# Seven block products for the up projection of two chunks, from the third token tile on

## The chip, the cores and the metric

One core of a Trainium2 chip runs the whole kernel. Its engines have instruction streams of their own and wait for one another by semaphores: TensorE (PE) multiplies and writes PSUM, with weight loads (PEld) beside the matmuls; VectorE (DVE), ScalarE (ACT) and GpSimd (POOL) do elementwise work, of which DVE and ACT read PSUM here; SyncE (SP) issues the DMAs. The metric is device microseconds of one execution, lower is better.

## The reference

Two softmax attentions (32 packed queries gather keys and values, then 576 queries read the packed result), the real part of a two-dimensional FFT, a layer norm, and a two-layer network with a ReLU:

```
p_packed = sm_attn(p, k, v)                    # 8 batches, 8 heads, 576 tokens, 64 per head
x = sm_attn(q, p_packed, p_packed)             # then (8, 576, 512)
mixed = np.real(np.fft.fft(np.fft.fft(x, axis=1), axis=2))
u = x + mixed
un = (u - mean(u)) / np.sqrt(var(u) + 1e-06)
out = u + np.maximum(un @ w_ch1, 0.0) @ w_ch2  # 512 -> 2048 -> 512
```

The change is in `un @ w_ch1` and in what surrounds it.

## The kernel before

The 4608 tokens are 36 blocks of 128, taken as nine tiles (t = 0 to 8) of 512. `front(b)` makes `u` of one batch: attention, FFT as matrix products, layer norm statistics. `ffn` runs the two-layer network of one tile. The 2048 hidden features are 16 chunks j of 128.

For each chunk `up` (L638) runs 12 matmuls of 128x512 into the PSUM bank `ph`, four blocks of 128 input features times three terms: each fp32 operand is a high and a low part (`uh`, `ul` for tokens, `wr_h`, `wr_l` for weights), and high·high, low·high and high·low are added. ACT makes `hh` = ReLU of `ph` (L644), DVE the low part `hl` (L645). `down` of the chunk before (L655) runs 12 matmuls into the four banks `acc0` to `acc3`. `wsplits` gives a weight chunk its high part on ACT (L101) and low part on POOL (L102), for w1 and w2, in every tile anew.

`step(i)` stands at two places in every chunk and runs the next piece of the front of batch t+1, in the order of the letters in `ORDER`, so that front and network of the tile before share the engines: `pz`, `py`, `px` are the front's FFT products (L228 to L230, L526), `pg`, `po`, `s`, `s2T`, `e1tp` its other PSUM results. Its PSUM tiles come from `bank`: three buffers of pool `ps`. From tile 1 on the order of PE, DVE, ACT and POOL is as the code is written (`manual_schedule`); in tile 0 a scheduler orders it. The front of batch 7 is issued in tile 6, its last pieces in tile 7, and tile 8 has none.

At the end of a tile the tokens of the next are centred (`less`, L592), transposed (L599, 16 matmuls into `untp`) and split into `uh` and `ul` by `parts`; `acc` times 1/σ plus `u` (L691) is the result, and SP stores it (L692). The PSUM has eight banks of 512 fp32: three of `ps`, `ph`, four `acc`.

Of the kernel before, what the change touches and what calls it, by code (L numbers as in the profile page):

```python
# [17 lines left out]
P = 128  # L18
S = 576
HS = S // 2  # L20
D = 64
# [21 lines left out]
         "y f1 r1 h1",  # L43
         "S y X y p0 p1 y d0 d1 y g0 y U y g1 y e0 y e1 y y m0 y a0 y m1 y a1 y f0 y r0 y h0 y f1 y r1 y "
         "h1 y y")

# [3 lines left out]
LEAD = 2  # L50
NJ = 16
MANUAL = {getattr(mybir.EngineType, n) for n in ("PE", "DVE", "Activation", "Pool")}
NE = 289
# [26 lines left out]
def tile_kernel(ctx, tc, kpT, qT, v, w1, w2, tabs, tabR, tabB, tabT, sel, ident_d, out):  # L80
# [6 lines left out]
    small = ctx.enter_context(tc.tile_pool(name="small", bufs=2))  # L87
    ps = ctx.enter_context(tc.tile_pool(name="ps", bufs=3, space=bass.MemoryType.PSUM))
    psf = ctx.enter_context(tc.tile_pool(name="psf", bufs=1, space=bass.MemoryType.PSUM))

    spare = ["acc0", "acc1", "acc2", "acc3"]
# [18 lines left out]
    for h in range(4):  # L110
        nc.gpsimd.memset(bmask[h * NPK:(h + 1) * NPK, h:h + 1], 0.5)
    w1f = cpool.tile([P, NJ, DM], F32, name="w1f")
    w2f = cpool.tile([P, NJ, DM], F32, name="w2f")

    nc.scalar.activation(small.tile([P, 1], F32, tag="ri", name="warm"), mhalf, AF.Exp)
    ubuf = cpool.tile([P, NU, DM], F32, name="ubuf")
    stages = (STG0 + STG1 * 40)[:2 * NJ]

# [24 lines left out]
    def spot(n, part, shape):  # L143

        t = (w1f, w2f)[n].rearrange("p j n -> p (j n)")[:, (part % NJ) * DM:]
        size = shape[1] * shape[2]
        return t[:, 0:size].rearrange("p (a n) -> p a n", a=shape[1])
# [12 lines left out]
    def load_weights(j):  # L160

        for n, dst in enumerate((w1f, w2f)):
# [5 lines left out]
            c = dst[:, j, :].bitcast(I32)  # L168
# [63 lines left out]
    def front(b):  # L232
# [56 lines left out]
        def turned_scores(*gs):  # L289
# [12 lines left out]
            for g in gs:  # L302
# [3 lines left out]
                rinv[g] = ri  # L306

        def packed(g):

# [42 lines left out]
        def queries(*gs):  # L352

            for g in gs:
                if g not in qts:
                    load_queries(g)

            tails = [bank("s2Tt")] + ([psf.tile([P, 512], F32, tag="ph", name="s2Tt")] if len(gs) == 2 else [])
            s2T = narrow(gs, lambda g, h: ppT[g][side(g, h):side(g, h) + D, h * NPK:(h + 1) * NPK],
                         lambda g, h, w: qts[g][side(g, h):side(g, h) + D, h // 2, w], "s2T", dict(zip(gs, tails)))  # L360
            for g in gs:
                s2s[g] = work.tile([P, 18, 32], F32, tag="att", name="s2", bufs=ATT)
            for c, w in ((1, slice(16, 18)), (0, slice(0, 16))):
                for g in reversed(gs):
                    nc.vector.transpose(s2s[g][:, w, :].rearrange("p a k -> p (a k)"), s2T[g][c])

        def less_one(g):
# [97 lines left out]
        def folded_parts(g):  # L465
# [12 lines left out]
        parts = {"S": lambda _: scores(0, 1), "U": lambda _: queries(0, 1), "X": lambda _: turned_scores(0, 1),  # L478
                 "s": scores, "t": turned_scores, "p": packed, "d": packed_parts, "q": queries, "e": less_one, "m": less_mean, "g": values_spectrum, "a": weights, "f": folded, "r": folded_rest,
                 "h": folded_parts,  # L480
# [10 lines left out]
        yh, yl, yr = [], [], []  # L491
        for t, base in enumerate((0, FO)):
            nr = NRC[t]
            hi = work.tile([P, 2, N2], F32R, tag="att", name="yh", bufs=ATT)
            lo = work.tile([P, 2, N2], F32R, tag="att", name="yl", bufs=ATT)
            for c in range(2):
                py = bank("py")
                for g in range(2):
                    w = slice(base + c * P, base + (c + 1) * P)
                    three(py[:, :N2], fh[g][:, w], fl[g][:, w], gh[g][:, t, :], gl[g][:, t, :], g == 0, g == 1)  # L500
                split(hi[:, c, :], lo[:, c, :], py[:, :N2])
            py = bank("pyr")
            for g in range(2):
                w = slice(base + 256, base + 256 + nr)
# [6 lines left out]
            yh.append(hi)  # L511
            yl.append(lo)
            yr.append(st)
            yield


        def spectrum(t, par):
# [63 lines left out]
    class Turned:  # L581
# [3 lines left out]

        def __init__(self, keys):
            self.keys, self.un, self.tp, self.hl = keys, {}, {}, None

        def less(self, i):
            key = self.keys[i]  # L590
            self.un[i] = work.tile([P, DM], F32, tag="ln", name="un")
            nc.vector.tensor_scalar(self.un[i], u_of[key], stat_of[key][:, 1:2], None, ALU.subtract)  # L592

# [9 lines left out]
        def parts(self, i):  # L603
            if self.hl is None:
                self.hl = [work.tile([P, 4, 512], F32R, tag=n, name=n, bufs=1) for n in ("uh", "ul")]
            w = slice(i * P, (i + 1) * P)
            split(self.hl[0][:, :, w], self.hl[1][:, :, w], self.tp[i].rearrange("p (c t) -> p c t", c=4))

    def wsplits():

        for _ in tiles:
            for n, j in [(0, 0)] + [x for j in range(1, NJ) for x in ((0, j), (1, j - 1))] + [(1, NJ - 1)]:
                hi = work.tile([P, DM], F32R, tag="wr", name="wr_h", bufs=6)
                lo = work.tile([P, DM], F32R, tag="wr", name="wr_l", bufs=6)
                split(hi, lo, (w1f, w2f)[n][:, j, :], nc.gpsimd)
                ready.append((hi, lo))
                yield

    def ffn(first, turned, step, nxt, alone):
        keys = turned.keys  # L620
        n = len(keys)
        T = n * P
        uh, ul = turned.hl
        acc = [psf.tile([P, DM], F32, tag=f"acc{i}", name=f"acc{i}") for i in range(n)]
        now["acc"] = acc

        def up(j, moves=(), between=lambda: None):
            moves = list(moves)
            wh, wl = ready.pop(0)

            pool, tag = (ps, "ps") if alone and j % 2 else (psf, "ph")
            ph = pool.tile([P, 512], F32, tag=tag, name="ph")

            step = T // 2 if first == 0 and j < SPL else T
            for t in (slice(i, i + step) for i in range(0, T, step)):
                for k in range(12):
                    c, (l, r) = k // 3, ((wh, uh), (wh, ul), (wl, uh))[k % 3]
                    nc.tensor.matmul(ph[:, t], l[:, c * P:(c + 1) * P], r[:, c, t], start=(k == 0), stop=(k == 11))  # L638
                    if moves:
                        moves.pop(0)()  # L640
            between()
            hh = work.tile([P, 512], F32R, tag="hh", name="hh")
            hl = work.tile([P, 512], F32R, tag="hl", name="hl")
            nc.scalar.activation(hh[:, :T], ph[:, :T], AF.Relu)  # L644
# [44 lines left out]
        for i, key in enumerate(keys):  # L689
# [3 lines left out]
            free.append(place_of[key])  # L693

    keys = []
    for b in range(B):
# [6 lines left out]
    for at in gen0:  # L703
        if at == "rest":
            break
    cur = Turned(tiles[0][1])
    for i in range(4):
# [4 lines left out]
    for _ in gen0:  # L712
        pass
    spare.clear()
    rest = iter(())
# [5 lines left out]
    for t, (first, tk) in enumerate(tiles):  # L721
# [14 lines left out]

        nxt = Turned(tiles[t + 1][1]) if t + 1 < len(tiles) else None

        with tc.manual_schedule(engines=MANUAL) if t > 0 else nullcontext():
            ffn(first, cur, step, nxt, t + 1 >= B)  # L740
        cur, rest = nxt, gen
# [112 lines left out]
```

## Time and profile before

| | |
|---|---|
| median of 3 runs | 1031.98 us (1029.85 to 1032.99) |
| the profiled execution | 1030.17 us, span 1028.4 us |
| granted clock, mean | 0.983 |
| instructions | 14863 |
| DMA | 59.10 MB, mean 57 GB/s |

The profile's parts are busy time per engine, forty slices of the span, the DMA queues, the chain of waits followed back from the last instruction, and groups of equal instructions (`out<-in`, count, busy us, mean ns, then idle time just before them and its releaser). A start and a duration are in us. The record of a matmul is longer than the distance to the next one, since matmuls are pipelined.

### The profile page before, as it was taken

Reading aid. Unit: us, or ns where it says so; the run is one execution under the profiler, and the core shown is the slowest. Engines: PE = TensorE matmul, PEld = TensorE weight load, DVE = VectorE, ACT = ScalarE, POOL = GpSimd, SP = SyncE. Lnnn points to the kernel's source line nnn. Section 1 sums busy time; section 2 is a strip of 40 time slices with the busy share of each in tenths; the row PEclk is TensorE's granted clock in tenths of the full one; section 3 lists DMA queues with packets and bytes.
Section 4 is the critical chain, followed back from the end, with each engine's and each line's share of the span. In section 5 each row is a group of like instructions: output and inputs, shape, how many; then the busy total and the mean of one; then the engine's idle time right before and its main releaser. Section 6 shows DMA issues by size and latency. Waiting matters only on the chain.

```text
span 1028.4 us, 14863 instructions
## 1 busy us (share of the span) xinstructions
PE 970.6 (94%) x5692; PEld 791.5 (77%) x5692; DVE 595.7 (58%) x1227; ACT 441.7 (43%) x910; POOL 469.8 (46%) x426
## 2 busy tenths in 40 slices
PE   4189889999999999999999999999999999999998
PEld 2167668878877888788877887788778888887886
DVE  4885963558465856577556846594658562114112
ACT  4577634444343434444444435444434443333321
POOL 3715644364335534454345533653455344544443
PEclk9599989999999999999999999999999999999999
DMA  9358400220023000310041002200210000001001
GB/s 360 118 180 277 140 1 1 93 96 1 1 67 121 1 1 29 111 50 1 1 139 49 1 1 93 96 1 1 86 54 1 1 35 7 1 0 41 1 1 42
DMA packets 18184, 59.10 MB, mean 57 GB/s; under 512 B 2166, under 2 KB 3008, under 8 KB 18112
## 3 DMA queue, kind: packets, MB, share of 16 engines
q1 hardware_dynamic: 17136, 56.70, 16.0%
q0 software_dynamic: 976, 1.44, 0.5%
q8 instruction: 45, 0.74, 0.3%
q14 instruction: 27, 0.22, 0.1%
HBM read 48.70 MB, written 9.44 MB: 57 GB/s over the span
## 4 chain that ended last, share of the span: by engine, by line
PE 78%; DVE 11%; ACT 5%; issue 2%; POOL 2%; DMA 1%; ACTq 0%; DVEq 0%; POOLq 0%
PE ph L638 35%; PE acc L655 31%; DVE turned L410 2%; DVE ubuf L558 1%; ACT hh L644 1%; DVE turned L406 1%; PE po L317 1%; PE s L260 1%; DMA ubuf<-w 1%; ACT junk L208 1%; POOL wr_l L102 1%; DVE hl L645 1%; PE py L228 1%; PE py L229 1%; PE py L230 1%
## 5 line engine op out<-in xcount | busy, mean ns | idle before, releaser
L102 POOL TENSOR_TENSOR wr_l<-w1f,wr_h 128x512 fp32r<-128x512 f32 x144 | 191.5, 1330 | 383.7 <-ACT wr_h L101 383.5
L645 DVE SCALAR_TENSOR_TENSOR hl<-ph,hh 128x512 fp32r<-128x512 f32 x144 | 98.9, 687 | 310.7 <-ACT hh L644 310.5
L638 PE MATMUL ph<-uh,wr_h 128*128 128x512 f32 (+1 forms) x580 | 231.1, 398 | 12.8 <-DVE hl L645 9.4
L102 POOL TENSOR_TENSOR wr_l<-w2f,wr_h 128x512 fp32r<-128x512 f32 x144 | 192.9, 1340 | 97.1 <-ACT wr_h L101 88.7
L655 PE MATMUL acc<-wr_l,hh 128*128 128x512 f32 x576 | 227.1, 394 | 3.0 <-POOL wr_l L102 3.0
L655 PE MATMUL acc<-wr_h,hh 128*128 128x512 f32 x576 | 227.9, 396 | 0.8 <-ACT hh L644 0.8
L638 PE MATMUL ph<-uh,wr_l 128*128 128x512 f32 (+1 forms) x580 | 228.5, 394 | 0.0
L638 PE MATMUL ph<-ul,wr_h 128*128 128x512 f32 (+1 forms) x580 | 228.3, 394 | 0.1
L655 PE MATMUL acc<-wr_h,hl 128*128 128x512 f32 x576 | 226.4, 393 | 0.0
L644 ACT ACTIVATE hh<-ph 128x512 fp32r<-128x512 f32 x144 | 85.9, 597 | 282.4 <-PE ph L638 282.3
L638 PEld LDWEIGHTS ph<-uh,wr_h 128*128 128x128 f32 x580 | 109.5, 189 | 48.0 <-DVE hl L645 11.4
L655 PEld LDWEIGHTS acc<-wr_l,hh 128*128 128x128 f32 x576 | 108.2, 188 | 26.9 <-POOL wr_l L102 5.4
L638 PEld LDWEIGHTS ph<-uh,wr_l 128*128 128x128 f32 x580 | 109.4, 189 | 24.0
L638 PEld LDWEIGHTS ph<-ul,wr_h 128*128 128x128 f32 x580 | 109.7, 189 | 22.9 <-DVE ubuf L575 0.8
L655 PEld LDWEIGHTS acc<-wr_h,hh 128*128 128x128 f32 x576 | 108.2, 188 | 24.6 <-ACT hh L644 1.0
L655 PEld LDWEIGHTS acc<-wr_h,hl 128*128 128x128 f32 x576 | 108.2, 188 | 23.2
L101 ACT CAST wr_h<-w1f 128x512 fp32r<-128x512 f32 x144 | 88.3, 613 | 14.5 <-PE acc L655 8.1
L101 ACT CAST wr_h<-w2f 128x512 fp32r<-128x512 f32 x144 | 89.4, 621 | 8.4 <-PE ph L638 6.7
L208 ACT ACTIVATE junk<-ubuf,stat 128x512 f32<-128x512 f32 x36 | 25.8, 719 | 74.1 <-DVE stat L204 74.1
L228 PE MATMUL py<-gh,fh 128*128 128x258 f32 x64 | 18.7, 294 | 27.4 <-ACT fh L470 27.4
L599 PE MATMUL untp<-ident,un 128*128 128x128 f32 x144 | 37.2, 273 | 0.9 <-DVE stat L211 0.8
L102 POOL TENSOR_TENSOR gl<-turned,gh 128x516 fp32r<-128x516 f32 x16 | 25.4, 1587 | 21.9 <-ACT gh L101 21.9
(197 smaller groups left out, 1306.4 us busy)
## 6 DMA issues: line engine op xcount, KB each, us to landing
kp<-kpT SPq DMA_DIRECT2D x16, 608.0 KB, 5.0
out<-ubuf SPq DMA_DIRECT2D x36, 256.0 KB, 2.1
vt<-v SPq DMA_DIRECT2D x14, 640.0 KB, 4.8
wst<-w SPq DMA_DIRECT2D x17, 512.0 KB, 4.7
qt<-qT SPq DMA_DIRECT2D x14, 576.0 KB, 4.9
ubuf<-w SPq DMA_DIRECT2D x9, 512.0 KB, 3.9
w1f<-w SPq DMA_DIRECT2D x3, 512.0 KB, 13.3
w2f<-w SPq DMA_DIRECT2D x3, 512.0 KB, 12.4
```

The costliest lines, as they stand in the source:

```text
L101: nc.scalar.copy(hi, src)
L102: (lo_eng or nc.vector).tensor_tensor(lo, src, hi.bitcast(F32), ALU.subtract)
L208: nc.scalar.activation(junk, u, AF.Square, bias=st[:, 1:2], scale=-1.0, accum_out=st[:, 2:3])
L228: nc.tensor.matmul(o, lh, rh, start=first, stop=False)
L229: nc.tensor.matmul(o, lh, rl, start=False, stop=False)
L230: nc.tensor.matmul(o, ll, rh, start=False, stop=last)
L410: TW[TA[min(b, 2)]].tensor_tensor(prod[0][:, t, :], prod[0][:, t, :], prod[1][:, t, :], ops[t])
L599: nc.tensor.transpose(tp[:, c * P:(c + 1) * P], un[:, c * P:(c + 1) * P], ident)
L638: nc.tensor.matmul(ph[:, t], l[:, c * P:(c + 1) * P], r[:, c, t], start=(k == 0), stop=(k == 11))
L644: nc.scalar.activation(hh[:, :T], ph[:, :T], AF.Relu)
L645: nc.vector.scalar_tensor_tensor(hl[:, :T], ph[:, :T], 0.0, hh[:, :T].bitcast(F32), ALU.max, ALU.subtract)
L655: nc.tensor.matmul(acc[i], l[:, w], r, start=(j == 0 and k == 0), stop=(j == NJ - 1 and k == 2))
```

## The change

Tiles 0 and 1 keep `up` and `down`. The two PSUM banks `ph` and `pb` are now halves of one tile `pair` of two banks, and pool `ps` has two buffers instead of three. In tiles 0 and 1 `bank` gives every third front tile `pb`; afterwards the front has the two `ps` buffers.

In tile 1 `combine` forms, for each pair m of chunks, the seven weight combinations of Strassen's scheme (three are blocks as they are, four are sums) as high and low parts, and writes them to DRAM `scratch`. Tiles 2 to 8 run `fast_ffn`. Its input, 512 tokens by 512 features, is cut in two by two; `Turned.parts` makes the token combinations T1 to T4 of the blocks in two parts (DVE, POOL, ACT), and B11, B21, B22 are blocks. A pair of chunks is seven products, each 6 matmuls of 128x256 (two blocks of 128 times three terms) into a quarter (256 columns) of `pair`. SP fetches the weights, a piece of 256 KB per product, into a ring of eight places in the room that w1 had. `begin`, `second` and `end` add the products up into four quarters of the pair's hidden values. `downs(m-1)`, 24 matmuls of 512 columns, stands between the fifth and sixth product of pair m. 1/σ is multiplied into the tokens by `less`, and `leave` adds `acc` to `u`. w1 is no longer split from tile 2 on. In some front pieces the order and the cut are new (`turned_block`, `queries_part`, `whole`, `remainder`).

```diff
+    pair = psf.tile([P, 2, 512], F32, tag="pair", name="pair")
+    ph, pb = pair[:, 0, :], pair[:, 1, :]
+    spare = ["acc0", "acc1", "acc2", "acc3", None]
...
-        if nbank[0] % 7 < 4 and spare:
-            return psf.tile([P, 512], F32, tag=spare[nbank[0] % 7], name=name)
+        n = nbank[0] % (2 + len(spare))
+        if n < len(spare):
+            return psf.tile([P, 512], F32, tag=spare[n], name=name) if spare[n] else pb
...
+    def fetch_piece():
+        if coming:
+            n, m, p = coming.pop(0)
+            at = piece(n)
+            nc.sync.dma_start(at.bitcast(F32), scratch[m][:, p, :, :])
+            ring.append(at)
...
+        def product(o, r, first=False):
+            w = ring.pop(0)
+            n = 0
+            for k in range(2):
+                for l, x in ((0, 0), (0, 1), (1, 0)):
+                    nc.tensor.matmul(o, w[:, l, k * P:(k + 1) * P], r[x][:, k, :], start=first and n == 0,
+                                     stop=n == 5, skip_group_check=not first)
+                    n += 1
+            fetch_piece()
...
+        def begin(m):
+            x = pair.rearrange("p b (a t) -> p b a t", a=2)
+            banks[m] = x
+            u3, u2 = sums[:, 2 * (m % 2)], sums[:, 2 * (m % 2) + 1]
+            product(x[:, 0, 0], B11, True)
+            nc.scalar.copy(u2, x[:, 0, 0])
+            product(x[:, 1, 0], T2, True)
+            nc.vector.tensor_tensor(u2, u2, x[:, 1, 0], ALU.add)
+            product(x[:, 0, 1], T1)
+            product(x[:, 0, 0], B21)
+            h, l = quarter(m, 0)
+            nc.scalar.activation(h, x[:, 0, 0], AF.Relu)
+            rest_of(h, l, x[:, 0, 0], nc.vector)
...
+            product(x[:, 1, 1], T3)
+            nc.vector.tensor_tensor(u3, u2, x[:, 1, 1], ALU.add)
+            nc.vector.tensor_tensor(u3, u3, x[:, 0, 1], ALU.add)
+            h, l = quarter(m, 2)
+            nc.scalar.activation(h, u3, AF.Relu)
+            rest_of(h, l, u3, nc.vector)
...
+            product(x[:, 0, 1], B22)
+            product(x[:, 1, 1], T4)
+            h, l = quarter(m, 1)
+            raw = sums[:, 2 * (m % 2):2 * (m % 2) + 2]
+            u2 = raw[:, 1]
+            nc.vector.tensor_tensor(raw, u2.unsqueeze(1).to_broadcast([P, 2, 256]), x[:, :, 1], ALU.add)
+            nc.scalar.activation(h, raw, AF.Relu)
+            rest_of(h, l, raw, nc.vector)
...
+        for m in range(1, M):
+            last = nxt is not None and m == M - 1
+            begin(m)
+            step(4 * m - 2)
+            second(m)
+            todo = sorted(downs(m - 1), key=lambda x: x[0])
+            run(todo, 8)
+            step(4 * m - 1)
...
+            step(4 * m)
+            run(todo, 2, [])
...
+            end(m)
...
+            step(4 * m + 1)
```

In the changed program these are lines 829 on; there L878 is the matmul of a product, L893 the copy in `begin`, L895 its add, L899 its ReLU, L906 and L907 the two adds after T3, L919 the add after T4, L884 `rest_of`, L936 a down, L798 and L814 the up and the down of tiles 0 and 1, L804 their `hl`, L762 the fetch of a piece.

The first place is PE in the last tile. Before, an up of a chunk and the start of the down of the chunk before it (brackets name the semaphores that an instruction waits for):

```order
L638 MATMUL ph<-uh,wr_h 128x512 [waits Activation_49]
L638 MATMUL ph<-ul,wr_h 128x512
L638 MATMUL ph<-uh,wr_l 128x512 [waits Pool_49]
L638 MATMUL ph<-uh,wr_h 128x512
L655 MATMUL acc_9385<-wr_h,hh 128x512 [waits Activation_49]
L655 MATMUL acc_9385<-wr_l,hh 128x512 [waits Pool_49]
L655 MATMUL acc_9385<-wr_h,hl 128x512 [waits DVE_49]
```

Now the first matmul of each product, from T4 of one pair on: T4, B11, T2, T1, B21, T3 and the first down (`uh` is B11 or B21, the `fast` buffers hold T1 to T4 and the pieces):

```order
L878 MATMUL pair<-fast_2984 128x256 [waits DMAHW3_49]
L878 MATMUL pair<-uh,fast_2984 128x256 [waits DMAHW4_49,DVE_49]
L878 MATMUL pair<-fast_2984,fast_2985 128x256 [waits DMAHW5_49,Activation_49]
L878 MATMUL pair<-fast_2984,fast_2985 128x256 [waits DMAHW6_49,DVE_49]
L878 MATMUL pair<-uh,fast_2983 128x256 [waits DMAHW7_49]
L878 MATMUL pair<-fast_2984,fast_2983 128x256 [waits DMAHW0_49,DVE_49]
L936 MATMUL acc_10423<-wr_h,hqh 128x512
```

Five of seven products wait for a PSUM reader (the sixth, B22, is behind the downs): B11 for L919, T2 for L893, T1 for L895, T3 for L884 of B21, B22 for L907. Between B11, T2, T1 and B21 stands nothing else.

The second place is DVE in the last tile. Before, its stream was one kind of instruction there, sixteen times:

```order
L645 SCALAR_TENSOR_TENSOR hl<-ph,hh 128x512 [waits Activation_49] x16
```

Now seven instructions serve one pair:

```order
L895 TENSOR_TENSOR sums<-sums,pair 128x256 [waits PE_49,Activation_49]
L884 SCALAR_TENSOR_TENSOR hql<-pair,hqh 128x256 [waits Activation_49]
L906 TENSOR_TENSOR sums<-sums,pair 128x256 [waits DVE_49,PE_49]
L907 TENSOR_TENSOR sums<-sums,pair 128x256 [waits DVE_49]
L884 SCALAR_TENSOR_TENSOR hql<-sums,hqh 128x256 [waits Activation_49]
L919 TENSOR_TENSOR sums<-sums,pair 128x512 [waits DVE_49,PE_49]
L884 SCALAR_TENSOR_TENSOR hql<-sums,hqh 128x512 [waits Activation_49]
```

What two instructions per two chunks did is now seven, four of which a later product waits for.

The third place is PE in tile 1. Before, the transposes `e1tp` wrote to a `ps` buffer, and the up after them waited for ACT:

```order
L294 MATMUL e1tp<-ident,e_1968 128x128 [waits PE_49]
L294 MATMUL e1tp<-ident,e_1968 128x128 x3
L294 MATMUL e1tp<-ident,e_1977 128x128 [waits Activation_49]
L294 MATMUL e1tp<-ident,e_1977 128x128 x3
L297 MATMUL e1tq<-ident,e_1968 64x128 [waits DVE_49]
L297 MATMUL e1tq<-ident,e_1977 64x128
L638 MATMUL ph<-uh,wr_h 128x512 [waits Activation_49]
```

Now half of them write to `pair`, wait for DVE (L804 of the up before), and the next up waits for ACT's read of them:

```order
L332 MATMUL e1tq<-ident,e_1919 64x128 [waits PE_49]
L332 MATMUL e1tq<-ident,e_1928 64x128
L347 MATMUL pair<-ident,e_1919 128x128 [waits DVE_49]
L347 MATMUL pair<-ident,e_1919 128x128 x3
L798 MATMUL pair<-uh,wr_h 128x512 [waits Activation_49]
```

In tile 1 some twelve of the front's pieces stand in `pair` between two ups.

More of the change, by code (lines that the diff above doesn't have):

```diff
@@ L365, in queries, with queries_part @@
                     nc.vector.transpose(s2s[g][:, w, :].rearrange("p a k -> p (a k)"), s2T[g][c])
+        def queries_part(c):
+            for g in range(2):
+                if g not in qts:
+                    load_queries(g)
+            part = {g: bank("s2T") for g in range(2)}
+            w = (slice(0, 512), slice(512, S))[c]
+            n = w.stop - w.start
+            for h in range(4):
+                for g in range(2):
+                    r, at = side(g, h), slice(h * NPK, (h + 1) * NPK)
+                    nc.tensor.matmul(part[g][at, :n], ppT[g][r:r + D, at], qts[g][r:r + D, h // 2, w],
+                                     start=True, stop=True, tile_position=(r, h * NPK))
+            for g in range(2):
+                if c == 0:
+                    s2s[g] = work.tile([P, 18, 32], F32, tag="att", name="s2", bufs=ATT)
+                to = s2s[g][:, w.start // 32:w.stop // 32, :]
+                nc.vector.transpose(to.rearrange("p a k -> p (a k)"), part[g][:, :n])
         def less_one(g):
@@ L510, in front @@
                                            ALU.mult, ALU.add)
-            yh.append(hi)
-            yl.append(lo)
             yr.append(st)
-            yield
+        for t in range(2):
+            yh.append(work.tile([P, 2, N2], F32R, tag="att", name="yh", bufs=ATT))
+            yl.append(work.tile([P, 2, N2], F32R, tag="att", name="yl", bufs=ATT))
+            whole(t, 0)
+            if t and b >= 2:
+                yield
+            whole(t, 1)
+            if t == 0 and b >= 2:
+                yield
+            remainder(t)
+            if t or b < 2:
+                yield
         def spectrum(t, par):
@@ L603, in parts @@
         def parts(self, i):
[L604 to L607, printed above, removed]
+            tp = self.tp[i].rearrange("p (c t) -> p c t", c=4)
+            if not self.fast:
+                h, l = (x.rearrange("p (c t) -> p c t", c=4)[:, :, i * P:(i + 1) * P] for x in (uh, ul))
+                split(h, l, tp)
+                return
@@ new lines, in parts @@
+            w = slice(i % 2 * P, i % 2 * P + P)
+            raw = extra("raw")
+            h, l = (x.rearrange("p (c t) -> p c t", t=256)[:, :, w] for x in (uh, ul))
+            if i < 2:
+                split(h[:, 0:4], l[:, 0:4], tp)
+                nc.scalar.copy(raw[:, :, w], tp)
+                return
+            top, low = tp[:, 0:2], tp[:, 2:4]
+            sh, sl = (x[:, :, :, w] for x in mixed())
+            r, q = (work.tile([P, 2, 2, P], F32, tag="tmp", name="mixraw", bufs=3) for _ in range(2))
@@ new lines, in parts, with extra, groups @@
+            nc.vector.tensor_tensor(l[:, 4:6], low, h[:, 4:6].bitcast(F32), ALU.subtract)
+            nc.scalar.copy(sh[:, 2:4], q)
+            nc.gpsimd.tensor_tensor(sl[:, 2:4], q, sh[:, 2:4].bitcast(F32), ALU.subtract)
+    extras = {}
+    def extra(name):
+        if name not in extras:
+            extras[name] = work.tile([P, 4, 256], F32, tag="wst", name=name, bufs=2)
+        return extras[name]
+    fast = {}
+    def groups():
+        if not fast:
+            for i in range(3):
+                fast[i] = work.tile([P, GROUPS[i + 1] - GROUPS[i], 512], F32R, tag=f"w1{i}", name=f"fast{i}", bufs=1)
+        return fast
@@ L617, in wsplits, with ffn @@
                 yield
-    def ffn(first, turned, step, nxt, alone):
+    def ffn(first, turned, step, nxt):
         keys = turned.keys
```

247 lines of the change are left out of this document (211 added, 36 removed).

## The prediction

> **What bounds the kernel now.** First the page: busy time, granted clock, the chain of waits.
>
> ```profile
> PE 970.6 (94%) x5692; PEld 791.5 (77%) x5692; DVE 595.7 (58%) x1227; ACT 441.7 (43%) x910; POOL 469.8 (46%) x426
> PEclk9599989999999999999999999999999999999999
> PE 78%; DVE 11%; ACT 5%; issue 2%; POOL 2%; DMA 1%; ACTq 0%; DVEq 0%; POOLq 0%
> L638 PE MATMUL ph<-uh,wr_h 128*128 128x512 f32 (+1 forms) x580 | 231.1, 398 | 12.8 <-DVE hl L645 9.4
> ```
>
> TensorE (PE) makes the end: 94% busy at nearly full clock, and its largest idle before any group is 12.8 us. What counts is therefore PE's stream: how many slots, and what stops it. Next the tiles, by the stores at each tile's end and by windows (busy us of PE, PEld, DVE, ACT, POOL, then clock).
>
> ```profile
> 735.53 2.31 SPq L692 DMA_DIRECT2D out<-ubuf  x4
> 844.55 180.07 SPq L692 DMA_DIRECT2D out<-ubuf  x12
> 408.60:517.60 109.00, 108.17 (x662) 88.92 (x661) 71.89 (x153) 47.18 (x100) 50.28 (x44) 1.00 0.13 45
> 735.50:844.50 109.00, 108.18 (x662) 88.92 (x661) 71.00 (x151) 46.46 (x98) 49.74 (x43) 1.00 0.10 33
> 844.50:945.00 100.50, 100.50 (x460) 82.79 (x459) 27.27 (x40) 32.34 (x61) 46.14 (x37) 1.00 0.06 22
> ```
>
> A tile that carries a front takes 109.0 us and PE is busy in 108.2 of them; in tile 7, without a front, PE never pauses. Inside it the chain in order of time gives the slots:
>
> ```profile
> 847.10 0.12 PE pz L228
> ...
> 848.66 0.12 PE pz L526
> ...
> 857.67 2.72 PE acc L655 x12
> 860.39 2.72 PE ph L638 x12
> ```
>
> Twelve 512-column matmuls are 2.72 us, 0.2268 a slot. Up and down of consecutive chunks alternate, so whatever reads one PSUM bank has 2.72 us of matmuls on other banks as cover. Fourteen pz matmuls (847.10 to 848.78) are 1.69 us.
>
> **What is removed.** Per pair of chunks 24 up matmuls of 512 columns give way to 42 of 256. The narrow slot is read from the front's products:
>
> ```profile
> 393.17 0.28 PE L228 MATMUL px<-bdh,xh 128*128 128x256 f32 x1
> ...
> 394.49 0.28 PE L230 MATMUL px<-bdh,ol 128*128 128x256 f32 x1
> 394.60 0.40 PE L655 MATMUL acc<-wr_h,hh 128*128 128x512 f32 x1
> ```
>
> Twelve in 394.60−393.17 = 1.43 us: 0.119 each, not half of 0.2268. A pair saves 24×0.2268 − 42×0.119 = 5.44 − 5.00 = 0.445 us, and 56 pairs (7 tiles × 8) save **24.9 us** (A). The Trainium skill, "TensorE: Matmul & The Clock Gate", section "Wait — 56ns, not 53.3ns?", has columns ÷ 2.4 GHz plus about 2.5 ns; worked out from it as an estimate, a pair saves 24×0.2158 − 42×0.1092 = 0.59 us, 33 in all. The row is 9% over the page for the narrow slot, and decides.
>
> **What is added: waits.** By the order of the changed program, each product waits for the last reader of any part of `pair`, not of its own quarter: T2 for the copy of B11's result (L893), T1 for the add that reads T2's (L895), T3 for the second half of the ReLU of B21's (L884), B22 for L907, and the next pair's B11 for the add over both banks (L919). B21 and T4 wait for nothing new. PE takes its queue in order: what stands behind a waiting product (T1, B21, then downs, which are ready) waits too. The price of a hand-over:
>
> ```profile
> 410.71 0.39 PE L638 MATMUL ph<-uh,wr_l 128*128 128x512 f32 x1
> ...
> 411.13 0.60 ACT L644 ACTIVATE hh<-ph 128x512 fp32r<-128x512 f32 x1 [3.44 <-PE ph L638]
> ...
> 411.77 0.69 DVE L645 SCALAR_TENSOR_TENSOR hl<-ph,hh 128x512 fp32r<-128x512 f32 x1 [1.23 <-ACT hh L644]
> ```
>
> ```profile
> 436.46 1.26 DVE L365 STREAM_TRANSPOSE s<-s2T 128x512 f32<-128x512 f32 x2
> ...
> 436.55 0.47 PE L638 MATMUL ph<-uh,wr_h 128*128 128x512 f32 x1 [0.33 <-DVE s L365]
> ```
>
> ```profile
> L528 ACT COPY spec<-pz 128x258 f32<-128x258 f32 x48 | 17.1, 373 | 16.8 <-PE pz L526 16.1
> L554 DVE TENSOR_TENSOR qe<-px,spec 128x256 f32<-128x256 f32 x16 | 6.6, 412 | 0.0
> ```
>
> A matmul's record runs past its slot: the narrow one lasts 0.28 in a slot of 0.119, 0.16 more. ACT starts 0.03 after the record's end (410.71+0.39 to 411.13), DVE 0.04 after ACT (411.13+0.60 to 411.77). Back to PE I take 0.03 too, an estimate: PE's row above starts after a grouped pair whose single end isn't shown. A 256-column read of PSUM is 0.37 on ACT, 0.41 on DVE, a 512-column one 0.69 on DVE. So where PE comes straight to the wait:
> - T4 to B11: 0.16+0.04+0.69+0.03 = 0.93 (C)
> - B11 to T2: 0.16+0.03+0.37+0.03 = 0.60, T2 to T1: 0.16+0.04+0.41+0.03 = 0.65 (B, 1.25 together)
> - B21 to T3: 0.16+0.03+0.38+0.04+0.41+0.03 = 1.06 (D)
>
> B22's is free while 24 downs (24×0.2268 = 5.44) stand ahead; in pair 0 there are none and it costs 1.1 (E). A pair loses up to 3.24 for the 0.445 it saves.
>
> Between B11, T2 and T1 the order puts nothing, in any tile: B = 56×1.25 = **70 us**. For C and D the front's own matmuls are placed between, in tiles 2 to 6 only: pz 1.69, px 1.43, others 0.5 to 0.9; they pay some waits. Over tiles 7 and 8: C 14×0.93 = 13 (seven passages from pair to pair in each), D 8×1.06 = 8.5 in tile 8 and 6.7 in tile 7, where the tail of a front still covers some, E 2.2. Counting by the order which waits in a front tile have something ahead, C is left with 5.5 and D with 4.1 per tile, ×5 = 27.5 and 20.5. C+D+E = **78 us**.
>
> **Late DVE.** In a front tile these adds queue behind the front's work on DVE, which until now only had to be done within a chunk:
>
> ```profile
> 455.77 0.76 DVE L416 TENSOR_TENSOR s<-s,z 128x576 f32<-128x576 f32 x1
> 456.56 0.78 DVE L418 STREAM_TRANSPOSE a<-s 128x576 f32<-128x576 f32 x1
> ...
> 458.60 0.38 DVE L385 TENSOR_SCALAR d<-z 128x18 f32<-128x18 f32 x1
> 459.01 1.23 DVE L386 TENSOR_SCALAR z<-z 128x18 f32<-128x18 f32 x1
> ```
>
> ```profile
> L410 DVE TENSOR_TENSOR turned<-turned 128x258 f32<-128x258 f32 x32 | 28.1, 916 | 0.4
> L474 DVE TENSOR_TENSOR ol<-eo,oh x16: 410/415/1535, 41.9 to 804.5; 128x256 fp32r<-128x256 f32 x16
> ```
>
> L416 and L418 (1.54 together) stand between L919 of one pair and L895 of the next, and two L410 (1.83) with more behind L895; pairs 3, 4, 5 and 7 have such stretches of 1.5 to 4.3 us ahead of a product, partly under matmuls. Nothing shows this directly: its bounds are 2 us a tile (all but one covered) and 14 (every stretch paid; a 256-column operation without PSUM swings from 410 to 1535 ns by L474). I take 6.8, in the middle, since half the stretches have downs ahead: 5×6.8 = **34 us** (F).
>
> **Boundaries and the first tiles.** At a tile's end B11 waits for a 512-column `ul` part on DVE (0.04+0.69+0.04 = 0.77), T2 for the mixed tokens of the fourth block (a chain over ACT, DVE and POOL, of which I count 1.36, three such steps less B11's time), and the last downs for the ReLU and the rest of the last pair (0.92): 3.05, seven times, **21 us** (G), bounds 5 and 35; it lies nearest to the lower hand-overs above, so I keep the sum. Tile 1 gives the front `pb`, the second half of the same two-bank tile: ups then wait for its readers and the front for L804 (`hl` from `ph`). The order shows twelve such waits, each one to two hand-overs (0.65 to 1.9), 1.3 on the mean, 15.6, and 2 for `combine` on DVE; tile 0 some 6 (automatic order). **23 us** (H), bounds 5 and 40.
>
> What before waits itself in tiles 2 to 8 is counted in these, about 5.6 us (0.8 in each of five front tiles by the windows, 1.6 at the end): −5.6 (I).
>
> POOL and ACT lose the splits of w1 in seven tiles; neither was the limit. The pieces:
>
> ```profile
> out<-ubuf SPq DMA_DIRECT2D x36, 256.0 KB, 2.1
> GB/s 360 118 180 277 140 1 1 93 96 1 1 67 121 1 1 29 111 50 1 1 139 49 1 1 93 96 1 1 86 54 1 1 35 7 1 0 41 1 1 42
> ```
>
> Seven of 256 KB per pair of about 13.7 us (10.44 of matmuls + 3.24) are 134 GB/s, under the 360 of the first slice; landing takes about 2.1 us, and eight are on the way, over a pair ahead. Cost 0; if SP holds a fetch back by more than that lead, each product waits about 2.1.
>
> **Sum**: −24.9 + 70 + 78 + 34 + 21 + 23 − 5.6 = +195.5, on the profiled execution's 1030.2 (span 1028.4): 1225.7, 1.8 below the median of runs, which is inside their spread. Forecast **1225 us**.
>
> **A rule against the waits.** Every matmul into `pair` here waits by whole tile. The Trainium skill, "PSUM — Partial Sum Buffer", section "PSUM bank collisions raise a hardware error", guards PSUM by bank × quadrant, by bank as the simple version. By it T2, T1 and T3 would find the bank's readers done, as the first rival works out.
>
> **Rivals.**
> - *Only the reader of the same bank holds a product back.* B11 and T2 use different banks, so T2 goes at once; T2's slot (6×0.119 = 0.71) then covers L893's 0.60, T1 and B21 cover L895, T3 is in the other bank. B goes, D goes, of F half: +195 − 70 − 38 − 17 = +70: **1100 us**. For it: the code uses four quarters in turn. Against: the order has a semaphore ahead of each. Chance 0.08, with all partly hidden cases from 1060 to 1165.
> - *DVE is the bound in front tiles.* If operations with `pair` run at L474's slow 1.5 instead of 0.41, eight pairs × four operations × 1.1 = 35 a tile where all are hit; half of them, 5×17 = 88: **1315 us**. For it: POOL still splits and mixes beside DVE; against: POOL's split work halves. Chance 0.08.
> - *Faster: hand-overs end before PE comes.* PE's sequencer could run ahead so that a product starts as its reader ends. The point is 0.445/4 = 0.11 us a wait, less than the 0.16 a record runs past its slot; only with waits near 0 and G, H, F gone does A stay: **1005 us**. Chance 0.02.
> - *The change doesn't act* (the pieces don't come earlier than needed): 7×2.1 a pair would be over 1285 and counts with the second.
>
> **Numbers.** Forecast 0.82, between 1165 and 1285: low with F, G and H at their low bounds (−24, −16, −18), high with F and G at theirs (+36, +14) and a little of H. Rivals 0.08, 0.08, 0.02. Under or over 0.3% (3 us, about what a measurement can tell): faster 0.02, within 0.01, slower 0.97.
>
> **What would show it.** PE's idle at L878 should be led by ACT L893 and DVE L895 with about 35 us each, by L919 and L884 with 25 to 45; tile periods of about 135 us with a front (109.0 + 26) and 118 in tile 7 (16×5.44 + 1.69 + 1.43 + 16 transposes of 0.12 = 92, and 26); clock still near 1.00. A tile 7 near 100 would speak for the rival by banks; L906, L907 or L895 of 1 us on the mean for the jam; idle at L878 led by DMA for late pieces. The forecast is wrong if hand-overs cost clearly less than 0.6, or if the downs of the pair before hide them.

## The result and the profile after

The changed kernel takes **1344.8 us** (median of 4 runs, 1334.36 to 1351.45) against 1031.16 before (4 runs, 1029.85 to 1032.99): 1.303 times as long, interval 1.294 to 1.313. The direction was as forecast; 313 us were lost where 195 were expected, and the time lies outside the range. The profiled execution took 1348.84 us with a span of 1347.0, 318.6 more than the span before.

The page of the changed kernel: busy time, granted clock by slices, the chain of waits.

```profile
PE 1080.1 (80%) x6700; PEld 884.4 (66%) x6700; DVE 691.8 (51%) x1581; ACT 445.0 (33%) x960; POOL 391.9 (29%) x364
PEclk8699998889897999889998997799988999996999
PE 47%; DVE 16%; ACT 5%; issue 3%; POOL 2%; DVEq 0%; ACTq 0%; POOLq 0%
```

PE is no longer always busy (94% before), and two things have happened: the clock, at 9 in every slice from the seventh on in the kernel before, is at 7 and 8 again and again, and DVE and ACT stand in the chain where PE stood. The waits of PE, by what it waited for (us in total, times, longest):

```profile
PE pair L878 <- DVE sums L895: 46.6, 56, 2.0
PE pair L878 <- DVE sums L919: 46.3, 34, 4.6
PE pair L878 <- ACT sums L893: 38.6, 50, 6.8
...
PE pair L878 <- DVE hql L884: 15.0, 17, 0.9
PE pair L878 <- DVE ul L884: 12.6, 18, 0.9
PE untp L676 <- DVE un L667: 9.0, 5, 1.8
```

These are the hand-overs B (L893, L895), C (L919) and D (L884) of the prediction. The chain in order of time shows one pair in the last tile, at full clock (start, us, what):

```profile
1291.69 1.44 PE pair L878 x12
...
1293.15 0.70 DVE sums L919
...
1293.89 1.00 PE pair L878 x6
...
1294.91 0.38 ACT sums L893
...
1295.34 0.99 PE pair L878 x6
...
1296.42 0.43 DVE sums L895
...
1296.89 1.71 PE pair L878 x12
...
1299.04 0.44 DVE ul L884
...
1299.52 0.98 PE pair L878 x6
1300.50 5.59 PE acc L936 x24
1306.09 1.44 PE pair L878 x12
```

One pair lasts 1306.09−1291.69 = 14.40 us, where two chunks took 4×2.72 = 10.88 before. Four times in a pair (ahead of B11, T2, T1 and T3) PE stands until DVE or ACT has read the product before. Windows of one tile each (busy us of PE, PEld, DVE, ACT, POOL, then the granted clock): tile 1, tile 3, tile 7, tile 8 (the last figures of a row are the DMA's share and GB/s).

```profile
194.90:352.10 157.20, 124.14 (x671) 95.86 (x669) 100.98 (x192) 56.55 (x112) 73.26 (x53) 0.93 0.38 129
511.20:657.80 146.60, 120.04 (x807) 100.26 (x806) 79.08 (x200) 46.00 (x107) 36.51 (x34) 0.93 0.43 134
1105.00:1226.40 121.40, 97.02 (x551) 80.39 (x550) 41.35 (x81) 29.25 (x61) 28.43 (x24) 0.99 0.43 129
1226.40:1339.80 113.40, 92.32 (x489) 76.97 (x489) 28.33 (x56) 21.60 (x44) 18.25 (x14) 0.92 0.37 109
```

Tile 7, at a clock of 0.99, comes to 121.4 against 118 expected. The misses are in the tiles with a front (tiles 2 to 6 take 145 to 159 us, 135 were expected) and in tile 1 (157; 127 expected, 110 before), and both have a lower clock.

How the clock is lost shows in windows of 3.41 us, PE alone (length, busy us and matmuls, granted clock), from the end of tile 7 on:

```profile
1219.99:1223.41 3.42, 1.81 (x13) 1.00 0.30 86
1223.41:1226.82 3.41, 2.48 (x13) 0.50 0.67 188
...
1237.06:1240.47 3.41, 2.48 (x12) 0.50 0.50 148
1240.47:1243.89 3.42, 3.42 (x11) 0.50 0.46 126
1243.89:1247.30 3.41, 3.41 (x16) 1.00 0.07 28
```

The waits of the first of these windows, from the timeline:

```profile
1221.21 0.38 PE L878 MATMUL pair<-fast,fast 128*128 128x256 f32 x1 [1.10 <-DVE fast L702]
1222.59 0.39 PE L878 MATMUL pair<-fast,fast 128*128 128x256 f32 x1 [0.51 <-DVE sums L895]
```

At the tile boundary, where waits for the mixed tokens (L702) meet those of a pair, PE is busy in 1.81 of 3.42 us, and the next window runs at half clock. It stays there for six windows (three are shown), though PE is busy in some 70% of each of the first five; only after the sixth, which is full (a pair's downs), does the clock return.

### The profile page after: what moved, and what is told of

Read it like the earlier page. It is cut to its first block, busy times and chain, and to the rows that moved or that the text cites. A ratio compares the mean times of both kernels' runs of the same rounds, so it can differ in the third digit from the quotient of the medians.

```text
span 1347.0 us, 18423 instructions
## 1 busy us (share of the span) xinstructions
PE 1080.1 (80%) x6700; PEld 884.4 (66%) x6700; DVE 691.8 (51%) x1581; ACT 445.0 (33%) x960; POOL 391.9 (29%) x364
## 4 chain that ended last, share of the span: by engine, by line
PE 47%; DVE 16%; ACT 5%; issue 3%; POOL 2%; DVEq 0%; ACTq 0%; POOLq 0%
PE pair L878 22%; PE acc L936 19%; DVE sums L919 2%; DVE hql L884 2%; DVE sums L895 2%; ACT hqh L920 1%; DVE ubuf L631 1%; DVE turned L469 1%; ACT sums L893 1%; DVE turned L473 1%; DVE ul L884 1%; ACT e L306 1%; POOL mixraw L700 1%; ACT uh L899 1%; ACT hqh L899 1%
## 5 line engine op out<-in xcount | busy, mean ns | idle before, releaser
L111 POOL TENSOR_TENSOR wr_l<-w2f,wr_h 128x512 fp32r<-128x512 f32 x144 | 197.3, 1373 | 577.4 <-ACT wr_h L110 508.7
L878 PE MATMUL pair<-fast,fast 128*128 128x256 f32 x1008 | 209.9, 316 | 88.8 <-DVE sums L895 38.4
L878 PEld LDWEIGHTS pair<-fast,fast 128*128 128x128 f32 x1008 | 163.4, 210 | 114.4 <-DVE sums L895 47.6
L878 PE MATMUL pair<-uh,fast 128*128 128x256 f32 x672 | 168.1, 310 | 48.2 <-DVE sums L919 46.3
L878 PEld LDWEIGHTS pair<-uh,fast 128*128 128x128 f32 x672 | 128.2, 210 | 63.4 <-DVE sums L919 53.3
L936 PE MATMUL acc<-wr_h,hqh 128*128 128x512 f32 x336 | 136.7, 407 | 5.3 <-ACT hqh L920 5.3
L936 PE MATMUL acc<-wr_h,hql 128*128 128x512 f32 x336 | 136.6, 407 | 0.0
L936 PE MATMUL acc<-wr_l,hqh 128*128 128x512 f32 x336 | 135.8, 404 | 0.0
L878 PE MATMUL pair<-fast 128*128 128x256 f32 x336 | 94.5, 320 | 31.1 <-ACT sums L893 10.0
L919 DVE TENSOR_TENSOR sums<-sums,pair 128x512 f32<-128x512 f32 x56 | 38.4, 686 | 155.6 <-PE pair L878 155.6
L878 PE MATMUL pair<-ul,fast 128*128 128x256 f32 x336 | 102.2, 304 | 2.8 <-DVE stat L232 2.3
L920 ACT ACTIVATE hqh<-sums 128x512 fp32r<-128x512 f32 x56 | 35.4, 632 | 185.7 <-DVE sums L919 185.7
L878 PEld LDWEIGHTS pair<-fast 128*128 128x128 f32 x336 | 66.9, 213 | 42.2 <-ACT sums L893 11.8
L884 DVE SCALAR_TENSOR_TENSOR hql<-sums,hqh 128x512 fp32r<-128x512 f32 (+1 forms) x84 | 50.7, 604 | 57.2 <-ACT hqh L920 43.6
L936 PEld LDWEIGHTS acc<-wr_h,hqh 128*128 128x128 f32 x336 | 64.4, 192 | 22.0 <-ACT hqh L920 8.4
L936 PEld LDWEIGHTS acc<-wr_h,hql 128*128 128x128 f32 x336 | 63.7, 190 | 19.2 <-issue 4.2
L878 PEld LDWEIGHTS pair<-ul,fast 128*128 128x128 f32 x336 | 70.7, 211 | 5.9 <-DVE stat L232 3.3
L798 PE MATMUL pair<-uh,wr_h 128*128 128x512 f32 (+1 forms) x132 | 56.0, 424 | 23.2 <-DVE hql L804 8.4
L936 PEld LDWEIGHTS acc<-wr_l,hqh 128*128 128x128 f32 x336 | 64.2, 191 | 13.8
L111 POOL TENSOR_TENSOR wr_l<-w,wr_h 128x512 fp32r<-128x512 f32 x32 | 44.3, 1385 | 88.3 <-ACT wr_h L110 88.2
L814 PE MATMUL acc<-wr_h,hqh 128*128 128x512 f32 x128 | 52.8, 412 | 3.9 <-ACT wr_h L110 2.2
```

The lines of the kernel that those rows point to most:

```text
L111: (lo_eng or nc.vector).tensor_tensor(lo, src, hi.bitcast(F32), ALU.subtract)
L814: nc.tensor.matmul(acc[i], l[:, w], r, start=(j == 0 and k == 0), stop=(j == NJ - 1 and k == 2))
L878: nc.tensor.matmul(o, w[:, l, k * P:(k + 1) * P], r[x][:, k, :], start=first and n == 0, stop=n == 5, skip_group_check=not first)
L884: eng.scalar_tensor_tensor(l, x, 0.0, h.bitcast(F32), ALU.max, ALU.subtract)
L919: nc.vector.tensor_tensor(raw, u2.unsqueeze(1).to_broadcast([P, 2, 256]), x[:, :, 1], ALU.add)
L920: nc.scalar.activation(h, raw, AF.Relu)
```

## The experiments

Two quantities go with each run: PE's idle time (span less PE's busy time) and what the clock takes (half of PE's busy time in stretches at half clock, since at full clock the same work needs half of it). Both are those of the profiled execution.

| run | median us | idle us | clock takes us |
|---|---|---|---|
| before | 1031 | 57.8 | 7.4 |
| changed | 1344.8 | 266.9 | 80.6 |
| e1_banks | 1147.3 | 138.3 | 30.0 |
| e2_between | 1210.3 | 178.4 | 55.3 |
| e3_both | 1160.4 | 143.4 | 48.6 |
| e4_warm | 1337.5 | 178.1 | 59.7 |
| e5_mix | 1146.5 | 141.5 | 31.9 |
| e6_nocombine | 1126.1 | 122.6 | 30.1 |
| e7_still | 1341.8 | 266.2 | 76.5 |
| e8_pool | 1158.7 | 138.7 | 41.6 |
| e9_relief | 1115.9 | 117.7 | 21.3 |
| e10_last | 1070.0 | 71.5 | 19.5 |
| e11_late | 1212.6 | 175.4 | 34.9 |

The theory of the guard: products wait because `pair` is guarded as one tile, and the waits thin PE's work out until the clock falls. What the clock takes is reckoned from the profile, not measured by switching it off. The theory's rivals: the supply (DVE, ACT or transfers cannot keep up), and narrow matmuls that lower the clock themselves.

### e1_banks: a tile for each bank

```diff
-    pair = psf.tile([P, 2, 512], F32, tag="pair", name="pair")
-    ph, pb = pair[:, 0, :], pair[:, 1, :]
+    ph = psf.tile([P, 512], F32, tag="ph", name="ph")
+    pb = psf.tile([P, 512], F32, tag="pb", name="pb")
...
-            x = pair.rearrange("p b (a t) -> p b a t", a=2)
+            x = [y.rearrange("p (a t) -> p a t", a=2) for y in (ph, pb)]
...
-            nc.vector.tensor_tensor(raw, u2.unsqueeze(1).to_broadcast([P, 2, 256]), x[:, :, 1], ALU.add)
+            for i in range(2):
+                nc.vector.tensor_tensor(raw[:, i], u2, x[i][:, 1], ALU.add)
```

> The two banks of `pair` are separate tiles, and the add after T4 is two 256-column adds; nothing else differs. Theory of the guard (waits by the whole two-bank tile cost some 245 us, and because they lie close together they bring the clock to one half for another 73): T2, T1 and T3 find their bank free, B11 waits 0.67 instead of 0.94 us after T4, tile 1 loses most of its waits on `pair`. Time 1090 to 1160 us, granted clock over 0.96, idle time of PE at the products under 70 us. Rival of supply (DVE, ACT or the pieces' DMA cannot keep up, and the waits only show it): the waits move to other instructions, time over 1280. Rival of the narrow matmul (the clock falls because of the 256-column matmuls and their weight loads): waits fall but the clock stays near 0.92, time about 1190.

Measured 1147.3 us, clock 0.961: 197 us come back from the tile declaration and one split instruction (how much the split alone gives was not run). The chain of a pair in the last tile is PE alone:

```profile
1093.45 5.59 PE acc L937 x24
1099.04 0.71 PE ph L878 x6
1099.76 0.71 PE pb L878 x6
1100.47 0.78 PE ph L878 x6
...
1104.36 5.59 PE acc L937 x24
```

A pair takes 1104.36−1093.45 = 10.91 us instead of 14.40. The products are the same; T2 ahead of T1, and T1 and B21 ahead of T3, now cover the readers. The theory of the guard holds; supply as the main limit and the narrow matmul fall: there are as many narrow matmuls, and the clock takes 30 us instead of 80.6. The last tile is within 2 us of before, but a tile with a front still takes 124 to 125 us instead of 109. PE's waits at the products sum to about 62 us, under 70 as expected, and half of that is one wait (of B11, for the first of the two adds after T4):

```profile
PE ph L878 <- DVE sums L920: 30.7, 15, 4.3
```

Fifteen waits, up to 4.3 us: e5, e8 and e9 follow them up.

### e2_between and e3_both: downs as cover

In `fast_ffn` the 24 downs of the pair before are placed into the waits, without (e2) and with (e3) separate banks. They are ordered so that those come first whose hidden quarters are ready (first and third quarter).

```diff
+        def begin(m, todo=()):
+            run(todo, 6)
...
             nc.scalar.copy(u2, x[:, 0, 0])
+            run(todo, 3)
             product(x[:, 1, 0], T2, True)
             nc.vector.tensor_tensor(u2, u2, x[:, 1, 0], ALU.add)
+            run(todo, 4)
...
             step(4 * m - 2)
+            run(todo, 5)
+            next(splits, None)
             second(m)
```

> `pair` stays one tile of two banks; the 24 downs of the pair before stand in the waits: 6 ahead of B11, 3 ahead of T2, 4 ahead of T1, 5 ahead of T3, 6 ahead of B22. Theory of the guard: 0.91 to 1.36 us of matmuls on other banks cover hand-overs of 0.62 to 1.09, in all pairs but a tile's first; tile 1 (157 us) stays as it is. Time 1110 to 1180, clock over 0.96. Rival of supply: DVE and ACT have the same work, so the time stays over 1280. Rival of the narrow matmul: about 1200 at a clock near 0.92.

> Separate banks and the downs in between. Theory of the guard: only the tile boundaries, the first pair of a tile and the front's late DVE work are left: 1040 to 1090, clock over 0.97, fast tiles with a front about 112, tile 7 about 94. Rival of supply: over 1250. Rival of the narrow matmul: about 1130 at a clock near 0.93.

Measured 1210.3 (clock 0.944) and 1160.4 (0.949). Both confirm that the waits can be covered, but they are 30 and 70 us over the range that the theory gave, e3_both even 13 over e1_banks. In the last tile e3_both does what was meant:

```profile
1095.69 1.39 PE acc L938 x6
1097.08 0.71 PE ph L878 x6
1097.79 0.70 PE acc L938 x3
...
1105.53 0.71 PE pb L878 x6
1106.24 1.39 PE acc L938 x6
```

10.55 us a pair, 0.33 under the kernel before: this is the gain of the seven products when nothing waits. In tiles with a front the wait came back elsewhere: B22, which has six downs ahead instead of 24, now waits for the second add after T3 (L910 there):

```profile
PE ph L878 <- DVE sums L910: 28.1, 18, 3.4
```

The five longest, 3.4 us, one in each tile with a front, each bring the clock down: in e3_both it takes 48.6 us, in e1_banks 30.0, and that is more than the 13 us between the two.

### e4_warm: the same waits, PE kept busy

```diff
+        def idle(n, go):
+            for _ in range(n if go else 0):
+                nc.tensor.matmul(acc[0][:, 0:256], zero, uh[:, 0:256], start=False, stop=False, skip_group_check=True)
```

> The changed kernel with matmuls of 128x256 by zero weights added to an `acc` in the waits: 4 ahead of T2, 4 ahead of T1, 7 ahead of T3 (from the third pair of a tile on), 6 behind T4. They add nothing to the result and fit into the waits (0.119 each). Theory that sparse stretches of 3.4 us bring the clock to one half: the waits stay, the clock of tiles 2 to 8 goes to 0.97 or more, and some 45 to 65 us of the 73 come back: 1280 to 1300. If the clock falls for another reason (narrow matmuls, load), it stays near 0.92 and the time is 1345 or above.

Measured 1337.5 us, clock 0.943; the clock takes 59.7 us, padding counted, instead of 80.6. The median is 7 us lower, where 45 to 65 had been expected, and that is inside the spread of the changed kernel (1334 to 1351), so no gain in time is shown; the 21 us that the clock takes less did not come out as time, and what the padding itself costs was not separated. What was wrong is which stretches are sparse enough: in the last tile, both the changed kernel (from 1243.9 us on) and this one (from 1232.8 on) keep the full clock in every ordinary pair, padded or not. The clock falls where a pair's waits meet another one, at tile boundaries, in the first pairs and behind late DVE work, and most of these places were not padded.

### e5_mix, e8_pool, e9_relief: what is left in the front tiles

These three start from e1_banks. e5_mix puts six downs ahead of B11 and leaves 18 behind T3. e8_pool makes the low parts of three hidden quarters on POOL. e9_relief leaves out the normalising of the second attention for batches 3 to 7 (so that its output differs there):

```diff
         def less_mean(g):
+            if b >= 3:
+                return
...
-            engs[g].tensor_tensor(s2s[g], s2s[g], broadcast(zs[g]), ALU.mult)
+            if b < 3:
+                engs[g].tensor_tensor(s2s[g], s2s[g], broadcast(zs[g]), ALU.mult)
```

> Separate banks as in the first experiment, and of the 24 downs six ahead of B11, the other 18 where they were (between T3 and B22). In e1_banks B11 still waited 30.7 us for the adds after T4, and in e3_both, with six downs left ahead of B22, B22 took over the wait (28.1 us). If cover is what counts, 1.4 us of downs take most of the short waits of B11, 18 downs still cover B22: 1115 to 1135. If DVE in the front tiles is itself full in pairs 3 to 5, the wait only moves: 1140 to 1160, as in the two others.

> Separate banks, and the low parts of the last three hidden quarters (half of u3, and both of the adds after T4: 256 and 512 columns) are made on POOL by a maximum and a subtraction in place of DVE: 1.1 us of DVE less per pair. If DVE's queue in the front tiles is what is left of the waits, the front tiles fall from 124.5 by 2 to 5 us each and the time by 10 to 25, to 1122 to 1137; tiles 7 and 8, without DVE pressure, stay or lose a little, since POOL takes longer and the downs that read these parts come later. If POOL beside DVE slows DVE's operations as in the rows of 1.5 us before the change, the time rises over 1150.

> Separate banks, and in the fronts of batches 3 to 7 DVE's normalising of the second attention is left out (the sums over 32, the reciprocal, and two passes over 576 columns for each of two groups; some 6 to 8 us of DVE per tile). If DVE is full in pairs 3 to 5 of a front tile (between 617 and 635 us of e1_banks it does not pause), so that the adds after T4 come up to 4.2 us late, the front tiles fall from 124.5 to 117 to 121 us, the wait of B11 from 30.7 to under 18, and the time by 15 to 40 us. If cover or order is what is missing, it stays within 8 of 1147.

e5_mix: 1146.5, no change against 1147.3; B11's wait falls to 8.9 us and the transposes, the splits of POOL and L698 take it over.

e8_pool: 1158.7, 11 slower. The low parts that DVE no longer makes took 63.6 us of it in e1_banks, but its busy time falls by 32 only (695.1 to 663.2): other operations last longer, L473 (no operand in PSUM) 948 ns on the mean instead of 667. That POOL's work does this is argued, not shown: in the changed kernel, with POOL no busier than in e1_banks, the same operation takes 774. Tiles 2 to 6 gain nothing; the loss is in tiles 7 and 8, which together take 191.3 us instead of 182.3. Downs now wait for POOL's low parts (6.6 us in the run), and the clock takes 41.6 us instead of 30.0.

e9_relief: 1115.9, 31 faster; a front tile takes 118.4 us instead of 124.5, and B11 waits 9.2 us instead of 30.7. So cover is not what is missing there: DVE is full in some pairs. (DVE's busy time falls by 35 us, hardly more than in e8_pool; what counts is where it falls.) Between 617 and 635 us of e1_banks (the third and fourth pair of a front tile) it runs almost without pause, and the add that B11 waits for comes some 4 us late, behind the normalising (timeline of DVE, then of PE):

```profile
630.26 0.71 DVE L447 TENSOR_REDUCE z<-s 128x18 f32<-128x576 f32 x1
...
631.97 1.19 DVE L449 TENSOR_SCALAR z<-z 128x18 f32<-128x18 f32 x1
...
633.37 0.70 DVE L451 TENSOR_TENSOR s<-s,d 128x576 f32<-128x576 f32 x1
633.99 0.41 DVE L920 TENSOR_TENSOR sums<-sums,ph 128x256 f32<-128x256 f32 x1
```

```profile
634.45 0.58 PE L878 MATMUL ph<-uh,fast 128*128 128x256 f32 x1 [4.21 <-DVE sums L920]
```

After that wait the first record is 0.58 long, where one behind a wait at full clock has 0.39: it brought the clock down as well.

### e6_nocombine: tile 1 without the combinations

e1_banks with the unmixed weights written to the scratch (tiles 2 to 8 then multiply by unmixed weights):

```diff
-        nc.vector.tensor_tensor(s[:, 0], s[:, 0], s[:, 2], ALU.subtract)
-        nc.vector.tensor_tensor(s[:, 2], s[:, 2], s[:, 3], ALU.add)
-        nc.vector.tensor_tensor(s[:, 3], s[:, 3], s[:, 0], ALU.subtract)
-        nc.vector.tensor_tensor(s[:, 1], s[:, 1], s[:, 3], ALU.subtract)
...
+        for i in range(2):
+            nc.sync.dma_start(scratch[m][:, 3:7, i, :], s)
```

> Separate banks, and in tile 1 the weight combinations are left out: the four sums per pair of chunks on DVE, the copy on ACT and the subtraction on POOL; unmixed weights go to the scratch in their place, so the products of tiles 2 to 8 are of wrong weights at the same cost. In e1_banks tile 1 takes 136 us where the kernel before takes 110. If DVE's some 26 us for the sums (they last 0.7 to 1.2 us each, 32 of them) delay the front in tile 1, its tile falls to 113 to 120, the time by 15 to 25. If the shared bank is what is left, tile 1 stays over 130.

Measured 1126.1, 21 us less; tile 1 falls from 136 to 122 us, the rest is in the tiles beside it. The combinations cost about 21 us, not the 2 that the prediction gave them. The edit leaves out their copy on ACT and their subtraction on POOL as well as the sums on DVE, and in tile 1 waits of PE for all three shrink: for L804 (DVE) from 5.0 to 2.2 us, for POOL's splits (L111) from 3.6 to 0.8, for ACT's `e1T` and mixed tokens (L350, L698) from 4.4 to nothing. Which engine costs most is not separated.

### e7_still: no stream of weights

The changed kernel fills the eight places of the ring once and uses them again and again, 384 transfers fewer.

```diff
-            nc.sync.dma_start(at.bitcast(F32), scratch[m][:, p, :, :])
+            if n < RING:
+                nc.sync.dma_start(at.bitcast(F32), scratch[m][:, p, :, :])
```

> The changed kernel with the pieces of weights fetched eight times only and then used again and again (wrong weights at the same cost): 384 transfers of 256 KB fewer. Theory of the guard: the time stays within 10 us of 1345, all waits stay. Rival of supply: over 50 us come back. Beside it: the 512-column slot is 0.233 us in the changed kernel and 0.227 before; if the transfers cause that, it goes back to 0.227, some 8 us.

Measured 1341.8, no difference: the 100 MB of pieces cost nothing, as predicted. The 512-column slot stays at 0.233 us, so it isn't the stream that lengthens it.

### e10_last and e11_late: the seven products in the last tile only

`FAST = 8`, in e3_both and in the changed kernel.

> Separate banks, downs in between, and the seven products in tile 8 only (FAST = 8): tiles 0 to 7 as the kernel before, with the weight combinations made in tile 7, where DVE has room. In e3_both tile 8 takes 85.7 us against 87.1 before. If the scheme pays for itself only where nothing else is on DVE, the time is 1028 to 1036 (no change that a measurement could tell); if the combinations or the two-bank front cost here too, 1040 to 1060.

> The changed kernel with FAST = 8: `pair` stays one tile of two banks, the seven products run in tile 8 only. Tiles 1 to 6 are then ups and downs with the front in the second half of `pair`. In tile 1 of the changed kernel that cost 21 us (157 against 136 with separate banks). If it costs as much in each of six or seven front tiles, 1031 + 6 to 7 times 15 to 21, and some 25 for tile 8: 1145 to 1200. If the 21 us came with the combinations alone, under 1100.

e10_last: 1070.0 us, ratio 1.037 (1.035 to 1.039), above both expectations. Tile 7, which now makes the combinations, takes about 106 us instead of 92. PE's waits in it (871.7 to 977.3 us) are for POOL's splits and, once, at the tile's end for the tokens; no up waits for DVE there:

```profile
PE acc L814 <- POOL wr_l L111: 4.2, 8, 0.8
PE pb L878 <- DVE ul L703: 3.9, 1, 3.9
```

Room on DVE was there, as expected, but the subtractions of the combinations (2.4 us each) stand on POOL right ahead of splits that downs wait for. PE is also busy 96.7 us instead of 91.8. Each front tile takes 112.8 on the mean instead of 109.0, an estimated 2 of it from the longer slots (384 × 0.005); PE also waits in each once for L804, 2.1 us. e11_late: 1212.6, 12 over the range expected; a front tile (2 to 6) takes 129.8 us on the mean against 112.8 with separate banks (e10_last). The shared two-bank tile alone costs 17 us in each, near the 15.6 of the prediction's H. No version tried is faster than the kernel before.

## Why the prediction was wrong in size

By its own steps:

- **A**, 24.9 us saved: right. With no wait a pair takes 10.55 us against 10.88 (e3_both); 0.33 instead of 0.445, the difference being the longer slot of the downs, 24×0.006.
- **The mechanism**, waits by the whole two-bank tile: right, and shown by e1_banks and, for the front's pieces, by e11_late against e10_last.
- **B, C, D, F** were 70, 40.5, 35.7 and 34, 180 us together. The waits for L893, L895, L919 and L884 are 38.6+46.6+46.3+27.6 = 159 us of idle time, and with the 0.16 that the record before each of the 175 waits runs past its slot, 187. E (1.9) fits too, and so does G: the waits for L667, L698, L702, L920 and the statistics at tile ends sum to 24 us (21 predicted).
- **The price of a wait** was 0.11 us too low. The first matmul behind a wait is followed by the next after 0.23 instead of 0.12 us:

```profile
1306.52 0.28 PE L878 MATMUL pair<-uh,fast 128*128 128x256 f32 x1
1306.64 0.28 PE L878 MATMUL pair<-fast 128*128 128x256 f32 x1
...
1308.29 0.39 PE L878 MATMUL pair<-uh,fast 128*128 128x256 f32 x1 [0.78 <-DVE sums L919]
...
1308.52 0.28 PE L878 MATMUL pair<-ul,fast 128*128 128x256 f32 x1
```

  175 waits × 0.11 = 19 us. The four hand-overs of the pair shown above, 0.94, 0.62, 0.75 and 1.09, are within 0.1 of 0.93, 0.60, 0.65 and 1.06. With them a pair comes to 42×0.119 + 24×0.233 + 3.40 + 4×0.11 = 14.43, and 14.40 were measured, where the prediction had about 13.7.
- **H**: tile 0 came to 5.5 (6 predicted). For tile 1 the shared bank was nearly right (15.6 predicted; 157 us against 136 with separate banks), the combinations were not: 21 us by e6_nocombine instead of 2. The step that failed is "2 for `combine` on DVE": 32 sums of 0.4 to 1.6 us on DVE were put at almost nothing, and the work on ACT and POOL at nothing. e10_last expected the same of tile 7, where POOL's part of it shows. Tile 1 without shared bank and combinations still takes 122 us against 110; what makes up these 12 was not separated.
- **The clock** is the step that failed worst. Every slot was priced at full clock, and the text expected it "still near 1.00". The clock takes 80.6 us where it took 7.4 before: 73 us. This is reckoned from busy time at half clock; no run removed it alone, and e4_warm, which took a quarter of it back, shows no clear gain in time.
- **The slots** of 512 columns are 0.233 us instead of 0.227, in tiles 0 and 1 also: about 12 us over all.

195.5 + 73 + 19 + 19 + 12 = 318.5, against 318.6 measured. That they meet so closely is luck: measured, B, C, D and F would add 7 and G 3, which the sum leaves out, and the 73 of the clock and the 19 of the combinations are not isolated by a run of their own. Which steps failed does not hang on it.

Of the rivals, the guard by banks is not what happens in this program (each product waits as the order shows), and is what e1_banks makes of it: 1147, where 1100 had been worked out without the clock and with half of F. The Trainium skill's rule in "PSUM — Partial Sum Buffer", section "PSUM bank collisions raise a hardware error", guards by bank and quadrant, by bank as the simple version; with the two tiles the trace agrees that this is enough: T2 starts 0.72 us after B11 (1099.04 to 1099.76 in e1_banks), right behind its six slots. DVE as the bound of front tiles was priced by slow operations (1.1 us more for half of them); what happens is that its queue is full in two or three pairs, some 6 us a tile (e9_relief).

## What to carry to other kernels

A tile is also a unit of waiting. Where several products rotate through parts of one PSUM tile, look in the order at what each waits for; here one declaration of two banks instead of two of one cost 197 us, eight times what the algorithm could save. When waits of half a microsecond come close together, price them with the clock in mind: ask how busy PE is in any stretch of 3.4 us, not only how long each wait is. And an engine that is 60% busy on the mean may have no room at the place where a new instruction goes.

## What the runs showed of the hardware

**The clock falls and returns at different loads.** PE's slots (a record cut at the next matmul's start, or by its overhang before a wait) were summed over windows of 3.413 us aligned with the clock's records, in the thirteen profiles:

```
clock at full: share of the window filled   next window at half
under 0.40                                  148 of 150
0.40 to 0.60                                 42 of 262
0.60 and over                                 0 of 3567
clock at half: share of the window filled   next window at full
under 0.75                                    0 of 179
0.75 to 0.80                                  3 of 24
0.80 and over                               199 of 208
```

In these profiles it falls after nearly every window less than 40% filled, after one in six between 40% and 60%, and never above; it returns after nearly every window more than 80% filled. Between 60% and 75% it stays as it is. That is why a kernel with waits in every pair can run long at half clock after a single bad window. The window shown above, some 45% filled by slots, lies in the band where it falls at times only. No wait of 3.4 us is needed: the longest in the window shown above is 1.10 us. The Trainium skill, "TensorE: Matmul & The Clock Gate", section "HAM oscillation — how this bites in real kernels", warns of idle gaps over about 3.4 us; the trace shows the clock falling with gaps a third as long, as that page's next section, "A second HAM failure mode: psum-queue depth-cycling", has it for frequent small gaps. These bands are observed, not set by an experiment; e4_warm moved the clock in the expected direction only (0.921 to 0.943).

**Slots of 512 columns** lasted 0.231 to 0.233 us on the median in all variants of the changed kernel, also without the stream (e7_still) and before any product ran, against 0.227 in the kernel before. What causes it stays open; where operands lie has changed, but that was not tried.
